# Two attention outputs behind one another on TensorE, and q's factor in its cast

## The chip, the cores and the metric

The kernel runs on one core of one Trainium2 chip. The metric is the device time of one execution in microseconds, the median of several runs. Everything that the profile shows comes from one profiled execution of the same program. PE is TensorE (PEld its weight loads), DVE is VectorE, ACT is ScalarE, POOL is GpSimd, SP is SyncE, which here only issues DMAs.

## The reference, cut to what matters

Attention with one added to the softmax denominator, then a feed-forward layer with the Mish-like gate. 8 batches, 12 heads, 448 positions, head width 64; the layer sees 3584 tokens of width 768, and its inner width is 2048.

```python
scores = scale * np.matmul(q, k.transpose(0, 1, 3, 2))          # scale = 1/8
m = np.max(scores, axis=-1, keepdims=True)
e = np.exp(scores - m)
attn = e / (np.sum(e, axis=-1, keepdims=True) + np.exp(-m) + 1e-09)
attn_out = np.matmul(attn, v)
x = attn_out.transpose(0, 2, 1, 3).reshape(3584, 768)
h = x @ w_in
g = h * np.tanh(np.log1p(np.exp(h)))                             # softplus inside
out = g @ w_out
```

## The kernel before, in words

**Pairs and units.** The 96 heads are taken two at a time: 48 pairs, six to a batch. Three pairs make a unit (`UNIT_PAIRS`), two units a batch; unit u has pairs 3u to 3u + 2, and `p0` is the first of them. Every instruction stands in the order in which the Python code writes it (the schedule is manual), so each engine runs its own instructions strictly in that order, and waits are put in by the framework from the data that instructions share.

**One pair** takes four steps. A step s computes scores of up to two blocks of 128 rows into the two banks of one of three PSUM tiles `sc` (PE, L327), takes the rows' maxima of both (DVE, L348), and exponentiates them into `en` (ACT, L361, with the sums collected at its side). The last step (s = 3) has one block only, so the second bank of its tile is free. `scores_ahead` keeps up to three steps of scores issued ahead of the exponentials; the scores of step n + 3 are therefore written right behind the exponentials of step n, into the tile that these set free. From pair 12 on the left operand is a block-diagonal copy of q, `qd` (`q_diag`, four buffers).

**The pair's output** (`av_pair`, L478) comes a unit later. It multiplies v by the transposed exponentials `eT`: eight matmuls, for two heads in two column halves of the array, into one PSUM bank, which VectorE copies to `xT` (L491). In the main units this output is written in front of the last score matmul of the pair three further on, in the free bank of the same `sc` tile (`av_with`, `bank=sc[:, 1, :]`): unit u computes the outputs of pairs p0 - 3, p0 - 2 and p0 - 1 at the last steps of its pairs p0, p0 + 1 and p0 + 2. `late` holds copies that are still to be written; `flush_late` writes them at the next chance, often the next step's start or the next part of the filler.

**The filler.** Between the steps PE works on the second matrix product of earlier batches (`mm2_part`, L567), in parts of sixteen matmuls of 384 or 192 columns. A part holds one of two PSUM tiles `mo` until VectorE has copied it to `o_sb` (L550). A list of weights, one for each of the unit's twelve steps, says which share of the unit's filler stands behind which step. After the twelve steps a unit has its share of the first matrix product (`mm1_mish`, L514 and L520), during which VectorE divides the exponentials by the denominators (`normalise`, L430), SP transposes them by DMA (L438, en to eT) and the next unit's first scores are issued.

**Loading.** SP issues the loads of q, k and v in float32 (L135), three buffers each. POOL casts them to bfloat16 (L186, `cast`). Up to pair 17 PE transposes q and k; from pair 18 (`BY_DMA_FROM`) two DMAs transpose three pairs at once (`turn_by_dma`, L197: k_cast to kT_all, q_cast to qT_all), and POOL writes both halves of each `qd` from qT_all, multiplying by 1/8 (L268). At a unit's first step POOL runs, in this order: a tiny copy that waits for the end of the previous normalisation (L714), the casts of v for pairs p0 - 2, p0 - 1 and p0, then k and q of the next unit's three pairs. The outputs of pairs p0 - 2 and p0 - 1 read v casts of this very list.

Of the kernel before, what the change touches and what calls it, by code (L numbers as in the profile page):

```python
# [12 lines left out]
ALU = mybir.AluOpType  # L13
AX = mybir.AxisListType

UNIT_PAIRS = 3
# [3 lines left out]
def kernel(  # L20
# [28 lines left out]
    STEPS = 4  # L49
# [65 lines left out]
    def flush_late():  # L115
        while late:
            late.popleft()()
# [10 lines left out]
    def load_pair(p, names="qkv"):  # L128
        if p >= N_PAIRS:
            return  # L130
        b, h0 = p // HP, (p % HP) * 2
        for nm in names:
            src = dict(q=q, k=k, v=v)[nm]
            t = ld_pool.tile([SP_, 2, NT * D], FP32, tag=f"{nm}_f", name=f"{nm}_f")
            nc.sync.dma_start(  # L135
                out=t, in_=src[b, h0 : h0 + 2].rearrange("h (p t) d -> p h (t d)", t=NT)
            )
            loaded.setdefault(p, {})[nm] = t
# [33 lines left out]
    def cast(p, names):  # L172
        if p >= N_PAIRS:
            return
        by_t = "p h (t d) -> p t h d"
        to = casted.setdefault(p, {})
        for nm in names:
            src = loaded[p].pop(nm)
            if nm != "v":
                to[nm] = (q_cast if nm == "q" else k_cast)[:, p % UNIT_PAIRS]  # L180
            else:
                to[nm] = bf_pool.tile([SP_, 2, NT * D], BF16, tag="v_bf", name="v_bf", bufs=7)
            if nm != "v":
                src = src.rearrange(by_t, t=NT)
            if p > 0 or nm == "v":
                nc.gpsimd.tensor_copy(out=to[nm], in_=src)  # L186
                continue
            cuts = (0, NT) if nm == "k" else (0, NT // 2, NT)
            for lo, hi in zip(cuts, cuts[1:]):
                nc.vector.tensor_copy(out=to[nm][:, lo:hi], in_=src[:, lo:hi])  # L190
# [42 lines left out]
    def evac_qk(p, act=False):  # L233
        if p >= N_PAIRS:
            return
        by_dma = p >= BY_DMA_FROM
        by = nc.gpsimd if by_dma else nc.vector
        kT = kT_all[:, p % (2 * UNIT_PAIRS)]
        (q_ps, k_ps), own = ((qT_all[:, p % UNIT_PAIRS], kT), []) if by_dma else qkT[p]
        mo_free.extend(own)  # L240
        q_reads = []
        qd = q_diag[p % len(q_diag)]
        if p < DIAG_FROM:
            qT = qd.rearrange("d i h r -> d (i h r)")[:, 0:S]
            qkT[p] = (qT, kT)
            if p == 0:
                nc.scalar.copy(kT, k_ps[:, 0:S])
                by_2 = sc_tiles[2][:, 0, :].bitcast(BF16)
                for ps, half in (q_ps, slice(0, S // 2)), (by_2, slice(S // 2, S)):
                    nc.vector.tensor_scalar(  # L250
                        out=qT[:, half], in0=ps[:, half], scalar1=SCALE, scalar2=None,
                        op0=ALU.mult,
                    )
                return
            if act:
                nc.scalar.mul(qT, q_ps[:, 0:S], SCALE)
            else:
                q_reads.append(nc.vector.tensor_scalar(
                    out=qT, in0=q_ps[:, 0:S], scalar1=SCALE, scalar2=None, op0=ALU.mult
                ))  # L260
        else:
            qkT[p] = (qd, kT)
            if p < DIAG_FROM + len(q_diag):
                nc.vector.memset(qd[0:64, :, 1, :], 0.0)
                nc.vector.memset(qd[64:128, :, 0, :], 0.0)
            for h in range(2):
                rows = slice(64 * h, 64 * h + 64)
                q_reads.append(by.tensor_scalar(  # L268
                    out=qd[rows, :, h, :],
                    in0=q_ps[rows, 0:S].rearrange("d (i r) -> d i r", i=QB),  # L270
                    scalar1=SCALE, scalar2=None, op0=ALU.mult,
                ))
        if by_dma:
            return
        if own and not act:
            nc.vector.tensor_copy(out=kT, in_=k_ps[:, 0:S])
        else:
            k_read = nc.scalar.copy(kT, k_ps[:, 0:S])
            if not own:
                apart(k_read, *q_reads)  # L280
# [26 lines left out]
    def scores(idx):  # L307

        p, s = divmod(idx, STEPS)
        if s == 0:  # L310
            if p < HP or p % UNIT_PAIRS == 0:
                for nm in ("negm", "sums", "expm", "den", "rden"):
                    stats[nm] = st_pool.tile([128, UNIT_PAIRS, NTILE], FP32, tag=nm, name=nm)
            at = 0 if p < HP else p % UNIT_PAIRS
            att[p] = {nm: t[:, at, :] for nm, t in stats.items()}
            att[p].update(en=en_bufs[p % N_EN], whole=dict(stats))
        st = att[p]
        qT, kT = qkT[p]
        kA, kB = kT[0:64, :], kT[64:128, :]
        sc = sc_tiles[idx % len(sc_tiles)]  # L320
        if s == STEPS - 1 and p in av_with:
            av_pair(av_with.pop(p), bank=sc[:, 1, :], beside=idx)
        if p >= DIAG_FROM:
            cols = tuple(range(2 * s, min(2 * s + 2, NTILE)))
            negm = st["negm"][:, cols[0] : cols[-1] + 1]
            for bk, i in enumerate(cols):
                nc.tensor.matmul(  # L327
                    sc[:, bk, 0:S], lhsT=qT[:, i].rearrange("d h r -> d (h r)"), rhs=kT,
                    start=True, stop=True,
                )  # L330
        elif s < 3:
            qa, qb = 128 * s, 64 + 128 * s
            nc.tensor.matmul(
                sc[:, 0, 0:S], lhsT=qT[0:64, qa : qa + 128], rhs=kA, start=True, stop=True
            )
            nc.tensor.matmul(
                sc[:, 1, 0:S], lhsT=qT[64:128, qb : qb + 128], rhs=kB, start=True, stop=True
            )
            cols, negm = (s, 4 + s), st["negm"][:, s : s + 5 : 4]
        else:  # L340
            nc.tensor.matmul(
                sc[0:64, 0, 0:S], lhsT=qT[0:64, 384:S], rhs=kA, start=True, stop=True
            )
            nc.tensor.matmul(
                sc[64:128, 0, 0:S], lhsT=qT[64:128, 0:64], rhs=kB, start=True, stop=True
            )
            cols, negm = (3,), st["negm"][:, 3:4]
        half_max[p] = nc.vector.tensor_reduce(  # L348
            out=negm, in_=sc[:, 0 : len(cols), 0:S], axis=AX.X, op=ALU.max, negate=True
        )  # L350
        st["sc", s] = (sc, cols)
# [250 lines left out]
            plan[u0 + 3] += [(g, 6, 2, 2)]  # L602


    weight = [5.2] + [1.0] * (steps - STEPS) + [0.4] * (STEPS - 1)

    LEAD = UNIT_PAIRS + 1
    LOAD_AT = (0, 3, 6)
# [61 lines left out]
    for u in range(UNITS_PER_B, N_UNITS + 2 * UNITS_PER_B):  # L670
        attn = u < N_UNITS
        filler = deque()
        for part in plan.get(u, []):
            filler.extend(mm2_part(*part))
        total, done, acc = sum(w for _, w in filler), 0, 0.0
        p0 = u * UNIT_PAIRS
        if attn and u >= first_mm2:
            av_with.update({p0 + i: p0 + i - UNIT_PAIRS for i in range(UNIT_PAIRS)})
        nxt = p0 + UNIT_PAIRS
        end = min(nxt, N_PAIRS) * STEPS  # L680

        for n in range(steps):
# [24 lines left out]
            if n in LOAD_AT and u <= first_mm2:  # L707
                at = p0 + LOAD_AT.index(n)
                load_pair(at + LEAD, "qk")
                load_pair(at + 1, "v")  # L710
                cast(at + LEAD - 1, "qk")
                cast(at, "v")
            elif n == 0 and u <= N_UNITS:
                nc.gpsimd.tensor_copy(  # L714
                    out=marks[0:1, 3, 0:2], in_=att[p0 - 1]["en"][0:1, NT - 1, NTILE - 1, 0:2]
                )
                for p_ in range(p0 - UNIT_PAIRS + 1, p0 + 1):
                    if "v" in loaded.get(p_, ()):
                        cast(p_, "v")
                for i in range(UNIT_PAIRS):  # L720
                    cast(nxt + i, "kq")
                turn_by_dma(nxt)
                load_pair(nxt + UNIT_PAIRS, "kq")
                for i in range(UNIT_PAIRS):
                    load_pair(p0 + 1 + i, "v")
            if s == 0 and u > first_mm2:
                evac_qk(nxt + pi)
            if n == steps - 1 and u >= first_mm2:
                for i in range(1, UNIT_PAIRS):
                    load_pair(nxt + UNIT_PAIRS + i, "kq")  # L730
            for pe, n0 in BY_PE.items():
# [27 lines left out]
        for f in range(FF_U):  # L759
# [6 lines left out]
            if f == 0:  # L766
                denominators(p0, UNIT_PAIRS)
                for p in todo if p0 < LATE_DIV else todo[:1]:
                    normalise(p, dma=p not in BY_PE)
            if f == 5 and u == UNITS_PER_B + 1:  # L770
                spread_rden(p0, copy=nc.scalar.copy)
            if f == 4:
# [42 lines left out]
```

## Time and profile before

| | |
|---|---|
| median of 3 runs | 471.48 us (470.95 to 472.93) |
| the profiled execution, whole | 475.91 us |
| its span, first to last instruction | 474.1 us |
| mean granted TensorE clock in it | 0.993 |
| busy: PE, DVE, ACT, POOL | 449.2, 347.5, 331.6, 180.8 us |
| DMA | 97.94 MB, mean 207 GB/s |
| one load of q, k or v | 224 KB, landing after 4.8 to 5.1 us (median) |

How to read it. A profile row such as "210.54 0.95 PE L478 MATMUL sc<-eT,v_bf 112*64 112x448 bf16 x8" is: start in us, time from the first start to the last end, engine, line, operation, output and inputs, shape, and how many instructions were merged. Matmuls overlap in the pipeline, so the distance from one row's start to the next is their cost on PE, not the second number. A bracket at a row's end tells how long the engine stood idle before it and whose end released it. In group rows the numbers behind the bar are total busy time and the mean of one in ns, then the idle time before them.

### The profile page before, as it was taken

The numbers are of one execution on the slowest core, as the hardware profiler recorded it, in microseconds if no ns is written. First come the engines' busy times: TensorE is split into PE (matmuls) and PEld (weight loads), VectorE is DVE, ScalarE is ACT, GpSimd is POOL, SyncE is SP. The second block draws the span as 40 slices with busy tenths as digits, with TensorE's granted clock in tenths as the row PEclk, the third lists the DMA queues.
The fourth block names the chain that finished last, engine by engine and source line by source line (L and its number), as shares of the span: only waits on it lengthen the run. The fifth ranks groups of instructions, "written<-read, shape, count | busy, mean of one in ns | idle before, by whom it ended". The sixth has DMA issues, their size and how long they took to land.

```text
span 474.1 us, 8841 instructions
## 1 busy us (share of the span) xinstructions
PE 449.2 (95%) x3051; PEld 245.8 (52%) x3051; DVE 347.5 (73%) x657; ACT 331.6 (70%) x877; POOL 180.8 (38%) x258
## 2 busy tenths in 40 slices
PE   7778888999889999999999999999999999999996
PEld 3344445555535555555555555555555555556563
DVE  5999738759859798989898888989798979421021
ACT  5998848879747887978686869687887869211300
POOL 4613609105126455455463644646464620100000
PEclk9999999999989999999999999999999999999999
DMA  8999999999999999999999999999999594921122
GB/s 253 228 115 244 220 216 209 174 214 252 185 239 280 222 273 231 261 250 230 259 233 287 212 224 242 282 233 268 217 273 235 155 213 128 225 76 33 35 57 77
DMA packets 232493, 97.94 MB, mean 207 GB/s; under 512 B 189312, under 2 KB 228992, under 8 KB 232448
## 3 DMA queue, kind: packets, MB, share of 16 engines
q1 hardware_dynamic: 224928, 91.06, 84.9%
q0 software_dynamic: 7488, 6.29, 9.2%
q8 instruction: 24, 0.39, 0.4%
q14 instruction: 21, 0.17, 0.1%
q10 hardware_dynamic: 32, 0.02, 0.0%
HBM read 45.61 MB, written 11.01 MB: 119 GB/s over the span
## 4 chain that ended last, share of the span: by engine, by line
PE 68%; ACT 6%; DVE 5%; DMA 3%; issue 1%; SPq 0%; DVEq 0%; ACTq 0%
PE mo L514 24%; PE mo L567 24%; PE sc L327 8%; PE sc L478 6%; ACT en L361 6%; DVE negm L348 4%; PE sc L514 4%; DMA eT<-en 3%; PE mo L478 1%; DVE xT L491 1%; PE mo L288 0%; DMA out_dram<-o_sb 0%; DVE o_sb L550 0%; PE sc L220 0%; DVE eT L453 0%
## 5 line engine op out<-in xcount | busy, mean ns | idle before, releaser
L361 ACT ACTIVATE en<-sc,negm 128x448 bf16<-128x448 f32 x336 | 208.8, 643 | 27.3 <-DVE negm L348 25.5
L348 DVE TENSOR_REDUCE negm<-sc 128x2 f32<-128x896 f32 x192 | 182.6, 970 | 50.2 <-PE sc L327 39.6
L567 PE MATMUL mo<-w_out_sb,gT 128*128 128x384 bf16 (+1 forms) x1024 | 167.4, 307 | 0.4 <-DVE rb L418 0.4
L514 PE MATMUL mo<-xT,w_in_sb 128*128 128x448 bf16 x672 | 139.0, 352 | 2.8 <-DMA w_in_sb<-in_moe_w_in_dram 2.6
L567 PEld LDWEIGHTS <-gT 128*128 128x128 bf16 x1024 | 96.6, 98 | 56.6 <-issue 2.9
L520 ACT ACTIVATE gT<-mo 128x448 bf16<-128x448 f32 x112 | 59.4, 543 | 82.2 <-PE mo L514 81.8
L514 PEld LDWEIGHTS <-w_in_sb 128*128 128x128 bf16 x768 | 74.0, 98 | 72.0 <-DMA w_in_sb<-in_moe_w_in_dram 3.8
L268 POOL TENSOR_SCALAR qd<-qT_all 64x448 bf16<-64x448 bf16 x60 | 80.1, 1335 | 61.7 <-DMA qT_all<-q_cast 32.6
L430 DVE TENSOR_SCALAR en<-en,rden 128x448 bf16<-128x448 bf16 x252 | 85.5, 413 | 0.5
L361 ACT ACTIVATION_READ_ACCUMULATOR en<-sc,negm 128x1 f32 x336 | 72.2, 215 | 0.0
L327 PE MATMUL sc<-kT_all,qd 128*128 128x448 bf16 x252 | 72.2, 356 | 0.0
L550 DVE COPY o_sb<-mo 128x384 f32<-128x384 f32 (+1 forms) x64 | 31.9, 498 | 48.3 <-PE mo L567 48.1
L478 PE MATMUL sc<-eT,v_bf 112*64 112x448 bf16 x336 | 40.2, 360 | 5.4 <-DMA eT<-en 3.6
L186 POOL CAST q_cast<-q_f 112x512 bf16<-112x512 f32 x47 | 28.6, 608 | 32.6 <-PE mo L409 18.6
L327 PEld LDWEIGHTS <-qd 128*128 128x128 bf16 x252 | 24.7, 98 | 29.2 <-issue 13.4
L714 POOL COPY marks<-en 1x2 bf16<-1x2 bf16 x12 | 2.1, 175 | 96.3 <-DVE en L430 96.3
L478 PEld LDWEIGHTS <-v_bf 112*64 112x64 bf16 x384 | 20.0, 109 | 24.1 <-issue 7.4
L186 POOL CAST k_cast<-k_f 112x512 bf16<-112x512 f32 x47 | 28.5, 607 | 0.6 <-DMA k_f<-in_k_dram 0.3
L186 POOL CAST v_bf<-v_f 112x512 bf16<-112x512 f32 x48 | 28.1, 605 | 1.5 <-DMA v_f<-in_v_dram 1.1
L514 PE MATMUL sc<-xT,w_in_sb 128*128 128x448 bf16 x96 | 20.8, 352 | 0.0
L491 DVE CAST xT<-sc 128x448 bf16<-128x448 f32 x33 | 20.3, 615 | 0.0
L520 ACT ACT_TABLE_LOAD x14 | 18.0, 1283 | 0.8 <-PE mo L514 0.3
(63 smaller groups left out, 245.2 us busy)
## 6 DMA issues: line engine op xcount, KB each, us to landing
k_f<-in_k_dram SPq DMA_DIRECT2D x48, 224.0 KB, 5.0
q_f<-in_q_dram SPq DMA_DIRECT2D x48, 224.0 KB, 4.8
v_f<-in_v_dram SPq DMA_DIRECT2D x48, 224.0 KB, 5.1
w_in_sb<-in_moe_w_in_dram POOLq DMA_DIRECT2D x12, 256.0 KB, 10.7
w_out_sb<-in_moe_w_out_dram POOLq DMA_DIRECT2D x8, 384.0 KB, 13.3
out_dram<-o_sb SPq DMA_DIRECT2D x7, 336.0 KB, 4.1
out_dram<-o_sb SPq DMA_DIRECT2D x8, 288.0 KB, 5.1
out_dram<-o_sb SPq DMA_DIRECT2D x8, 240.0 KB, 3.7
```

The costliest lines, as they stand in the source:

```text
L186: nc.gpsimd.tensor_copy(out=to[nm], in_=src)
L268: q_reads.append(by.tensor_scalar(out=qd[rows, :, h, :], in0=q_ps[rows, 0:S].rearrange("d (i r) -> d i r", i=QB), scalar1=SCALE, scalar2=N ...
L327: nc.tensor.matmul(sc[:, bk, 0:S], lhsT=qT[:, i].rearrange("d h r -> d (h r)"), rhs=kT, start=True, stop=True,)
L348: half_max[p] = nc.vector.tensor_reduce(out=negm, in_=sc[:, 0 : len(cols), 0:S], axis=AX.X, op=ALU.max, negate=True)
L361: e = nc.scalar.activation(out=st["en"][:, :, c, 0:SP_], in_=sc[:, bk, 0:S].rearrange("q (j c) -> q j c", j=NT), func=AF.Exp, bias=st["neg ...
L430: nc.vector.tensor_scalar(out=en[:, :, i, 0:SP_], in0=en[:, :, i, 0:SP_], scalar1=st["rden"][:, i : i + 1], scalar2=None, op0=ALU.mult,)
L478: mm = nc.tensor.matmul(av[h * 64 : (h + 1) * 64, 0:S], lhsT=v_bf[:, h, j * D : (j + 1) * D], rhs=e_h, start=(j == 0), stop=(j == NT - 1),)
L491: read = nc.vector.tensor_copy(out=to, in_=av[:, 0:S])
L514: nc.tensor.matmul(h_ps[:, 0:S], lhsT=w_in_sb[:, dm, ff * 128 : (ff + 1) * 128], rhs=xT[b][:, dm, :], start=(dm == 0), stop=(dm == DM_T - 1),)
L520: nc.scalar.activation(out=gT[:, ff, b % 2 * S : b % 2 * S + S], in_=h_ps[:, 0:S], func=AF.Mish)
L550: nc.vector.tensor_copy(out=o_sb[:, cols.start : cols.start + n_dve], in_=st["o"][:, 0:n_dve])
L567: nc.tensor.matmul(st["o"][:, 0:n_cols], lhsT=gT[:, ff, i * 128 : (i + 1) * 128], rhs=w_out_sb[:, ff, cols], start=(ff == 0), stop=(ff == ...
```

## The change

From unit 5 to unit 15 (pairs 15 to 47) the first of a unit's three outputs no longer stands at the first pair's last step. It stands at the second pair's last step, directly in front of the second output, in a `mo` tile of its own, and its copy is written at once. The third output stays at the third pair's last step. In these units the filler's weights are changed.

From pair 18 on the factor 1/8 moves from POOL's writes of `qd`, which become plain copies, into POOL's cast of q, which becomes a `tensor_scalar`. At a unit's first step POOL casts k and q of the next unit first, and then v.

In unit 4 the loads of q and k for pairs 19 and 20 are issued behind the first normalisation and its transpose instead of ahead of them, at the last step.

```diff
@@ cast
+            if nm == "q" and p >= BY_DMA_FROM:
+                nc.gpsimd.tensor_scalar(
+                    out=to[nm], in0=src, scalar1=SCALE, scalar2=None, op0=ALU.mult
+                )
+                continue
             if p > 0 or nm == "v":
                 nc.gpsimd.tensor_copy(out=to[nm], in_=src)
                 continue
@@ evac_qk
-                q_reads.append(by.tensor_scalar(
-                    out=qd[rows, :, h, :],
-                    in0=q_ps[rows, 0:S].rearrange("d (i r) -> d i r", i=QB),
-                    scalar1=SCALE, scalar2=None, op0=ALU.mult,
+                q_h = q_ps[rows, 0:S].rearrange("d (i r) -> d i r", i=QB)
+                if by_dma:
+                    nc.gpsimd.tensor_copy(out=qd[rows, :, h, :], in_=q_h)
+                    continue
+                q_reads.append(nc.vector.tensor_scalar(
+                    out=qd[rows, :, h, :], in0=q_h, scalar1=SCALE, scalar2=None, op0=ALU.mult,
                 ))
@@ scores
         if s == STEPS - 1 and p in av_with:
-            av_pair(av_with.pop(p), bank=sc[:, 1, :], beside=idx)
+            *in_mo, in_sc = av_with.pop(p)
+            for other in in_mo:
+                av_pair(other)
+                flush_late()
+            av_pair(in_sc, bank=sc[:, 1, :], beside=idx)
@@ the weights
-    weight = [5.2] + [1.0] * (steps - STEPS) + [0.4] * (STEPS - 1)
+    weight_first = [5.2] + [1.0] * (steps - STEPS) + [0.4] * (STEPS - 1)
+    weight_joint = [5.2] + [1.4] * 3 + [1.0] * 4 + [0.6] + [0.4] * 3
@@ the units' loop
+        weight = weight_joint if first_mm2 < u < N_UNITS else weight_first
         p0 = u * UNIT_PAIRS
         if attn and u >= first_mm2:
-            av_with.update({p0 + i: p0 + i - UNIT_PAIRS for i in range(UNIT_PAIRS)})
+            done_at = (0, 1, 2) if u == first_mm2 else (1, 1, 2)
+            for i, at in enumerate(done_at):
+                av_with.setdefault(p0 + at, []).append(p0 + i - UNIT_PAIRS)
...
+                for i in range(UNIT_PAIRS):
+                    cast(nxt + i, "kq")
                 for p_ in range(p0 - UNIT_PAIRS + 1, p0 + 1):
                     if "v" in loaded.get(p_, ()):
                         cast(p_, "v")
-                for i in range(UNIT_PAIRS):
-                    cast(nxt + i, "kq")
                 turn_by_dma(nxt)
...
-            if n == steps - 1 and u >= first_mm2:
+            if n == steps - 1 and u > first_mm2:
                 for i in range(1, UNIT_PAIRS):
                     load_pair(nxt + UNIT_PAIRS + i, "kq")
...
                 for p in todo if p0 < LATE_DIV else todo[:1]:
                     normalise(p, dma=p not in BY_PE)
+                if u == first_mm2:
+                    for i in range(1, UNIT_PAIRS):
+                        load_pair(nxt + UNIT_PAIRS + i, "kq")
```

More of the change, by code (lines that the diff above doesn't have):

```diff
@@ L236, in evac_qk @@
         by_dma = p >= BY_DMA_FROM
-        by = nc.gpsimd if by_dma else nc.vector
         kT = kT_all[:, p % (2 * UNIT_PAIRS)]
```

## The prediction

> **What bounds the kernel now.** I read the page first, then the stretches, then the order of time on each engine.
>
> ```profile
> span 474.1 us, 8841 instructions
> PE 449.2 (95%) x3051; PEld 245.8 (52%) x3051; DVE 347.5 (73%) x657; ACT 331.6 (70%) x877; POOL 180.8 (38%) x258
> ...
> 120.00:146.00 26.00, 22.42 (x141) 12.04 (x140) 18.15 (x35) 16.41 (x45) 6.38 (x10) 0.93 1.20 214
> ...
> 197.00:222.40 25.40, 25.30 (x158) 13.87 (x157) 22.85 (x44) 20.39 (x56) 13.67 (x18) 1.00 1.04 259
> ```
>
> The columns of a stretch are its length, busy PE, PEld, DVE, ACT and POOL, then granted clock, DMA share, GB/s. A unit (three pairs; unit 8 here) takes 25.4 us and PE is busy in 25.3 of it: PE bounds, and every wait put into PE's stream is lost for good. VectorE, at 22.85 us, is close behind. Only unit 5 (120 to 146 us) has a hole.
>
> PE in unit 8 (pairs 24 to 26), with the steps that the change moves; L478 is an attention output, L327 scores, L567 the filler:
>
> ```profile
> 207.19 3.41 PE L567 MATMUL mo<-w_out_sb,gT 128*128 128x384 bf16 x20
> 210.54 0.95 PE L478 MATMUL sc<-eT,v_bf 112*64 112x448 bf16 x8
> 211.42 0.36 PE L327 MATMUL sc<-kT_all,qd 128*128 128x448 bf16 x1
> ...
> 214.70 0.81 PE L567 MATMUL mo<-w_out_sb,gT 128*128 128x384 bf16 x4
> 215.47 0.95 PE L478 MATMUL sc<-eT,v_bf 112*64 112x448 bf16 x8
> 216.35 0.36 PE L327 MATMUL sc<-kT_all,qd 128*128 128x448 bf16 x1
> 216.55 0.81 PE L567 MATMUL mo<-w_out_sb,gT 128*128 128x384 bf16 x4
> 217.20 0.54 PE L327 MATMUL sc<-kT_all,qd 128*128 128x448 bf16 x2
> 217.57 0.81 PE L567 MATMUL mo<-w_out_sb,gT 128*128 128x384 bf16 x4
> ...
> 220.39 0.95 PE L478 MATMUL sc<-eT,v_bf 112*64 112x448 bf16 x8
> ```
>
> Starts to starts: four filler matmuls take 0.65 us, two scores 0.38, one 0.19, an attention output 0.88. Going into an output costs more: 214.70 + 0.65 is 215.35, and it starts at 215.47, 0.12 late; and its 0.88 is 0.13 above four pairs of 448 columns at 0.19 each (two matmuls run side by side). So a separate output costs some 0.24 us of changing over.
>
> The third output starts where a chain ends, not where PE is ready:
>
> ```profile
> 216.81 0.62 DVE L348 TENSOR_REDUCE negm<-sc 128x1 f32<-128x448 f32 x1 [0.29 <-PE sc L327]
> 217.35 0.62 DVE L491 CAST xT<-sc 128x448 bf16<-128x448 f32 x1
> 217.89 3.10 DVE L348 TENSOR_REDUCE negm<-sc 128x2 f32<-128x896 f32 x3
> ...
> 219.00 0.63 ACT L361 ACTIVATE en<-sc,negm 128x448 bf16<-128x448 f32 x1 [0.51 <-DVE negm L348]
> ...
> 220.14 0.20 ACT L361 ACTIVATION_READ_ACCUMULATOR en<-sc,negm 128x1 f32 x1
> ```
>
> Last score of the second pair (216.35), its maximum (216.81), the output's copy (217.35), the third pair's first maximum (217.89), its two exponentials (219.00 to 220.34), then the third output in the bank they free (220.39): 4.04 us. PE's own work there is about 3.87, so 0.17 is already waited. PE and this chain are level.
>
> **Joining the outputs.** In units 5 to 15 the first output leaves the front of the first pair's last score and stands directly before the second. One change-over goes: 11 x 0.24 = 2.6 us. No matmul is added. What follows, in unit 8, from the score that now comes first (210.44, the 20 fillers at 0.1625 from 207.19):
>
> The filler weights put two more filler matmuls (0.33 us) between the first and the second pair's last score, and two fewer behind. PE asks for the second pair's first scores at 211.3 but their tile is free only when the first pair's second step is exponentiated:
>
> ```profile
> 211.29 0.21 ACT L361 ACTIVATION_READ_ACCUMULATOR en<-sc,negm 128x1 f32 x1
> ```
>
> It ends at 211.50, PE goes on at 211.55: 0.26 us waited, which the output hid before. The first output now needs a mo bank. In even units the filler part that held it has just ended, the copy out of it stands behind a maximum on VectorE, and by the same latencies PE waits another 0.13. So the second pair's last score starts at 216.35 - 0.24 + 0.26 + 0.13 + 0.33 = 216.83. From there PE has 3.54 us of work to the third output (a score 0.19, ten fillers 1.63, six half-wide ones 0.49, three times two scores 1.14, changing over 0.09); the chain still takes 4.04. The third output starts at 220.87 instead of 220.39, with the same work done: **+0.48 us in an even unit**, although the gap went.
>
> An odd unit:
>
> ```profile
> 235.88 0.95 PE L478 MATMUL sc<-eT,v_bf 112*64 112x448 bf16 x8
> ...
> 241.69 0.36 PE L327 MATMUL sc<-kT_all,qd 128*128 128x448 bf16 x1
> ...
> 245.74 0.95 PE L478 MATMUL sc<-eT,v_bf 112*64 112x448 bf16 x8
> ...
> 243.23 1.08 DVE L348 TENSOR_REDUCE negm<-sc 128x2 f32<-128x896 f32 x1
> 244.23 0.55 DVE L550 COPY o_sb<-mo 128x384 f32<-128x384 f32 x1
> 244.69 2.08 DVE L348 TENSOR_REDUCE negm<-sc 128x2 f32<-128x896 f32 x2
> ```
>
> Without the output in front, its first pair's last score starts at 235.71. The same steps (-0.24, 0.24 waited, 0.33 of filler) bring the second pair's last score to 242.02. But the filler part now ends two matmuls behind it, so that in VectorE's order the copy to o_sb (0.46, 244.23 to 244.69) comes ahead of the third pair's first maximum instead of behind it: the chain, 4.05 now, becomes 4.51, against 3.70 of work on PE (fourteen fillers). Third output at 246.53 instead of 245.74: **+0.79**. The first output's own copy has slack.
>
> **q's factor in its cast, and v's casts behind k's and q's.** This sits on POOL:
>
> ```profile
> L268 POOL TENSOR_SCALAR qd<-qT_all 64x448 bf16<-64x448 bf16 x60 | 80.1, 1335 | 61.7 <-DMA qT_all<-q_cast 32.6 <-PE sc L327 13.5 <-PE sc L478 12.0
> L186 POOL CAST q_cast<-q_f 112x512 bf16<-112x512 f32 x47 | 28.6, 608 | 32.6 <-PE mo L409 18.6 <-DMA q_f<-in_q_dram 13.9
> ...
> L389 POOL CAST hl<-rden 128x7 bf16<-128x7 f32 x6 | 1.1, 191 | 12.7 <-DVE rden L385 12.2 <-PE mo L409 0.5
> ...
> 210.27 0.17 POOL L714 COPY marks<-en 1x2 bf16<-1x2 bf16 x1 [5.76 <-DVE en L430]
> 210.40 1.70 POOL L186 CAST v_bf<-v_f 112x512 bf16<-112x512 f32 x3
> 212.05 0.60 POOL L186 CAST k_cast<-k_f 112x512 bf16<-112x512 f32 x1
> 212.60 0.60 POOL L186 CAST q_cast<-q_f 112x512 bf16<-112x512 f32 x1
> ...
> 235.71 1.70 POOL L186 CAST v_bf<-v_f 112x512 bf16<-112x512 f32 x3
> ```
>
> Sixty multiplies become copies and thirty casts become multiplies of 112x512. No row shows that one. Bounds: 0.608 us, the plain cast of the same data, and the multiply at L268's rate: 0.18 us fixed (7 columns take 0.191), (1.335 - 0.18) / 448 = 2.58 ns a column, so 1.50 us for 512. I take 1.50, as the same operation; casts follow each other 0.05 closer than they last.
>
> What waits: the second output reads the v cast first among this unit's three. It is done at 211.0 now and used at 215.47. Afterwards, from 210.40: three k casts at 0.55, three q at 1.45, then v in 0.60: 217.0. PE is there at 216.0. The output starts at 217.07, the score behind it at 217.95, the third output 4.04 later at 221.99: **+1.60 in an even unit**, the 0.48 included. Odd, with the casts from 235.71: the second output at 242.38, the score at 243.26, plus 4.51 is 247.77: **+2.03**. Up to a multiply of about 1.1 us nothing is added to 0.48 and 0.79. Units 6 to 14 cast both; unit 15 has no k and q left, unit 5's second output uses an older v.
>
> [...]
>
> The copies into qd, between 0.53 (the cast's rate) and 1.33 us, are covered either way: at 1.33 they are ready in time now. With POOL shorter there, VectorE's normalisation is less disturbed; PE waits for no eT in steady units, so I price this at nothing.
>
> ```profile
> 215.00 1.92 SPq L197 DMA_TRANSPOSE kT_all<-k_cast  x1
> 217.03 1.55 SPq L197 DMA_TRANSPOSE qT_all<-q_cast  x1
> ```
>
> SP's transposes of k and q are issued at these times now, behind the unit's eT. Their third casts would be done at 215.0 (k) and 216.4 (q): no shift.
>
> **The loads of pairs 19 and 20.** Unit 5:
>
> ```profile
> 132.66 1.38 PE L478 MATMUL sc<-eT,v_bf 112*64 112x448 bf16 x8 [3.58 <-DMA eT<-en]
> ...
> 144.12 0.95 PE L478 MATMUL sc<-eT,v_bf 112*64 112x448 bf16 x8
> ...
> L438 SPq DMA_TRANSPOSE eT<-en x3: 3738/3873/12086, 118.3 to 134.4; - x3
> ...
> DMA to landing us min/median/max: 6.4/6.8/14.3
> ```
>
> The first of the three takes 12.1 us to issue and lands at 132.6, 14.3 after 118.3; PE waits 3.58 us for it. Four loads now go behind this transpose instead of ahead, so it lands sooner, by an estimated 2 to 3 us. The second stays behind all of the same transfers: issued at 130.4 and landed 6.4 later, at 136.8; afterwards 137 to 139, because the queue runs empty for an estimated 1 to 2 us before 118.3. With the join the second output follows the first at once. PE gets there at 132.66 - 3.58 + 4.3 (fillers and scores) + 0.9 (first output) = 134.3 and waits for the second eT instead. At 138, the third output comes at 138 + 0.88 + 4.51 = 143.4 instead of 144.12: **-0.7**, between -2.7 (136) and +0.8 (139.5). The 3.58 us hole is moved rather than closed.
>
> **Sum.** 5 x 1.60 + 4 x 2.03 + 0.79 (unit 15) - 0.7 = +16.2 us. The profiled execution took 475.91 (its span and 1.8 around it): 492.1. The runs' median is 4.4 lower, in the whole run: 471.48 + 16.2 = **487.7 us**.
>
> **Rivals.** *The multiply is quick*, at most 1.1 us: no v wait, only the chain is left, 5 x 0.48 + 5 x 0.79 - 0.7 = +5.7, 477.2 us. For it: plain casts run at 0.608. Against: L268. Between 1.1 and 1.45 us lie 478 to 487. [...]
> *Faster: the change-over decides.* The multiply is quick and the third output finds its bank free, because VectorE, relieved of POOL or in another order, gets through the chain in under 3.5 us: -2.6, and -0.7 to -2.7 in unit 5: 466.2 to 468.2. Against it stands 4.04 us in rows that the change doesn't touch; it decides only where at least 0.5 us of that goes.
> *The parts cancel*: chain +0.3 a unit, unit 5 at its best: within 2.4 us of 471.5.
>
> **How the numbers follow.** The multiply near 1.5: 0.50; in between: 0.10; quick with the chain: 0.18; cancelling: 0.06; faster: 0.16. A measurement tells about 0.5% (2.4 us) from no change. Slower 0.78, same 0.06, faster 0.16. Likeliest case alone: 483 to 492 (multiply 1.4 to 1.6, unit 5's bounds). Leaving out the faster case and a tail: 471 to 491.5.
>
> **What would show it.** POOL's q multiply by its mean; PE waiting for POOL's v cast before the second output, 9 times about 1 us; the third output waiting for ACT 0.4 to 0.8 us in every unit from 6; units of 26.9 (even) and 27.3 us (odd) instead of 25.3; unit 5's wait at its second output, for eT. A multiply under 1.1 us, or third outputs without a wait, would make the forecast wrong.

## The result and the profile after

| | before | after |
|---|---|---|
| median | 471.22 us (469.15 to 472.93) | 487.44 us (486.12 to 491.94) |
| the profiled execution, whole | 475.91 us | 491.72 us |
| ratio of the times, 95% interval | | 1.0375 (1.0317 to 1.0433) |

The change makes the kernel slower by 3.75%, 16.2 us between the medians; 487.7 us was forecast. Some executions of a kernel take over 1.5% longer than its fastest: the medians here and below count them, the ratios leave them out. The page after:

```profile
span 489.6 us, 8838 instructions
...
PE 452.6 (92%) x3051; PEld 248.4 (51%) x3051; DVE 329.6 (67%) x657; ACT 334.3 (68%) x877; POOL 161.4 (33%) x258
```

VectorE and GpSimd are *less* busy (347.5 and 180.8 us before). TensorE has the same 3051 matmuls, 3.4 us more busy time, and its share falls from 95 to 92%. So most of the time was not added as work; it went into waits. The place is read from stretches cut from third output to third output, units 8 and 9, first of the kernel before and then of the one after (length, PE, PEld, DVE, ACT, POOL):

```profile
sum 50.65, PE 50.55 PEld 27.63 DVE 44.88 ACT 40.43 POOL 26.76; mean PE 25.27 PEld 13.81 DVE 22.44 ACT 20.22 POOL 13.38
```

```profile
197.25:224.16 26.91, 25.36 (x151) 13.59 (x151) 20.13 (x43) 20.46 (x54) 10.90 (x16) 1.00 0.91 228
224.16:251.55 27.39, 25.49 (x163) 14.28 (x163) 20.56 (x44) 20.36 (x54) 12.57 (x20) 1.00 0.92 230
sum 54.30, PE 50.86 PEld 27.88 DVE 40.70 ACT 40.82 POOL 23.47; mean PE 25.43 PEld 13.94 DVE 20.35 ACT 20.41 POOL 11.73
```

The lengths are those forecast, 26.9 us for an even and 27.3 for an odd unit (before 25.30 and 25.35); two units take 3.65 us more, at a granted clock of 1.00 in both kernels. In unit 8 TensorE's order of time has two holes that were not there (first the two joint outputs, then the score, then the third output), and GpSimd's shows why the first is there:

```profile
217.32 0.95 PE L488 MATMUL mo<-eT,v_bf 112*64 112x448 bf16 x8
219.23 0.95 PE L488 MATMUL sc<-eT,v_bf 112*64 112x448 bf16 x8 [0.97 <-POOL v_bf L191]
220.11 0.36 PE L337 MATMUL sc<-kT_all,qd 128*128 128x448 bf16 x1
...
224.16 0.95 PE L488 MATMUL sc<-eT,v_bf 112*64 112x448 bf16 x8 [0.43 <-ACT en L371]
```

```profile
212.43 0.17 POOL L728 COPY marks<-en 1x2 bf16<-1x2 bf16 x1 [13.02 <-DVE en L440]
212.55 0.60 POOL L191 CAST k_cast<-k_f 112x512 bf16<-112x512 f32 x1
213.12 1.48 POOL L186 TENSOR_SCALAR q_cast<-q_f 112x512 bf16<-112x512 f32 x1
...
218.58 1.71 POOL L191 CAST v_bf<-v_f 112x512 bf16<-112x512 f32 x3
```

The first of the three v casts ends at about 219.18; without a wait the second output starts 0.76 us after the first (experiment 1), which is 218.1 here. Over the whole run, in the view of waits (us in all, times, longest):

```profile
PE sc L488 <- POOL v_bf L191: 9.2, 9, 1.1
PE sc L488 <- ACT en L371: 7.0, 13, 0.7
PE sc L488 <- DMA eT<-en: 1.9, 1, 1.9
```

Nine waits for v, as many as there are units 6 to 14. The multiply and its neighbours among the groups of instructions:

```profile
L440 DVE TENSOR_SCALAR en<-en,rden 128x448 bf16<-128x448 bf16 x252 | 64.1, 332 | 0.5
...
L186 POOL TENSOR_SCALAR q_cast<-q_f 112x512 bf16<-112x512 f32 x30 | 44.4, 1478 | 0.0
L274 POOL COPY qd<-qT_all 64x448 bf16<-64x448 bf16 x60 | 33.3, 556 | 29.6 <-DMA qT_all<-q_cast 24.7
```

### The profile page after: what moved, and what is told of

It is laid out like the page before. It is cut to its first block, busy times and chain, and to the rows that moved or that the text cites. A ratio compares the mean times of both kernels' runs of the same rounds, so it can differ in the third digit from the quotient of the medians.

```text
span 489.6 us, 8838 instructions
## 1 busy us (share of the span) xinstructions
PE 452.6 (92%) x3051; PEld 248.4 (51%) x3051; DVE 329.6 (67%) x657; ACT 334.3 (68%) x877; POOL 161.4 (33%) x258
## 4 chain that ended last, share of the span: by engine, by line
issue 28%; PE 25%; POOL 18%; DMA 5%; DVE 4%; ACT 2%; SPq 1%; POOLq 0%; DVEq 0%
PE mo L577 10%; PE mo L524 8%; POOL q_cast L186 8%; POOL qd L274 6%; DMA qT_all<-q_cast 5%; POOL k_cast L191 3%; DVE negm L358 2%; PE sc L488 2%; ACT en L371 2%; PE sc L337 2%; PE sc L524 1%; PE mo L488 1%; POOL v_bf L191 1%; DVE o_sb L560 1%; SPq L448 1%
## 5 line engine op out<-in xcount | busy, mean ns | idle before, releaser
L371 ACT ACTIVATION_READ_ACCUMULATOR en<-sc,negm 128x1 f32 x336 | 70.2, 209 | 0.0
L440 DVE TENSOR_SCALAR en<-en,rden 128x448 bf16<-128x448 bf16 x252 | 64.1, 332 | 0.5
L488 PE MATMUL sc<-eT,v_bf 112*64 112x448 bf16 x248 | 30.0, 363 | 18.2 <-POOL v_bf L191 9.2
L186 POOL TENSOR_SCALAR q_cast<-q_f 112x512 bf16<-112x512 f32 x30 | 44.4, 1478 | 0.0
L274 POOL COPY qd<-qT_all 64x448 bf16<-64x448 bf16 x60 | 33.3, 556 | 29.6 <-DMA qT_all<-q_cast 24.7
L337 PEld LDWEIGHTS <-qd 128*128 128x128 bf16 x252 | 24.6, 98 | 28.0 <-issue 13.0
L191 POOL CAST q_cast<-q_f 112x512 bf16<-112x512 f32 x17 | 10.5, 616 | 25.6 <-PE sc L337 17.2
```

Of the source, the lines that this page charges most:

```text
L186: nc.gpsimd.tensor_scalar(out=to[nm], in0=src, scalar1=SCALE, scalar2=None, op0=ALU.mult)
L274: nc.gpsimd.tensor_copy(out=qd[rows, :, h, :], in_=q_h)
L337: nc.tensor.matmul(sc[:, bk, 0:S], lhsT=qT[:, i].rearrange("d h r -> d (h r)"), rhs=kT, start=True, stop=True,)
L371: e = nc.scalar.activation(out=st["en"][:, :, c, 0:SP_], in_=sc[:, bk, 0:S].rearrange("q (j c) -> q j c", j=NT), func=AF.Exp, bias=st["neg ...
L440: nc.vector.tensor_scalar(out=en[:, :, i, 0:SP_], in0=en[:, :, i, 0:SP_], scalar1=st["rden"][:, i : i + 1], scalar2=None, op0=ALU.mult,)
L488: mm = nc.tensor.matmul(av[h * 64 : (h + 1) * 64, 0:S], lhsT=v_bf[:, h, j * D : (j + 1) * D], rhs=e_h, start=(j == 0), stop=(j == NT - 1),)
```

## The experiments

All kernels in one table. "Two units" is the distance between the third outputs of units 7 and 9 in the profiled execution, repeated within 0.1 us by each later two units up to unit 15 (in the kernel after and in 3 up to unit 13: unit 15 casts no k and q, and units 14 and 15 together take 53.04 and 52.25 us there). It tells more than the medians, since the executions of one kernel scatter by one or two per cent here (what is known of that is said at the fifth experiment).

| kernel | ratio to before (95%) | two units, us |
|---|---|---|
| before | 1 | 50.65 |
| after | 1.0375 (1.0317 to 1.0433) | 54.30 |
| 1 after, v cast first | 1.0123 (1.0031 to 1.0216) | 51.88 |
| 2 after, q's cast plain | 1.0168 (1.0031 to 1.0305) | 51.88 |
| 3 before + factor in q's cast, v last | 1.0325 (1.0247 to 1.0403) | 53.83 |
| 4 before + joint outputs | 1.0182 (1.0083 to 1.0281) | 51.90 |
| 5 before + later loads | 0.9996 (0.9942 to 1.0051) | 50.64 |
| 6 joint outputs, old weights | 1.0158 (1.0071 to 1.0245) | 52.21 |
| 7 as 6, copy later | 1.0178 (1.0116 to 1.0241) | 52.80 |
| 8 before + copy later | 1.0050 (1.0005 to 1.0095) | 51.23 |
| 9 as 4, copy later | 1.0109 (1.0051 to 1.0166) | 51.65 |
| 10 filler moved, copy later | 1.0028 (0.9971 to 1.0085) | 50.99 |
| 11 filler moved | 1.0107 (1.0033 to 1.0181) | 51.51 |
| 12 filler moved less, copy later | 0.9989 (0.9952 to 1.0027) | 50.93 |

**1. The changed kernel with v's casts first.**

```diff
-                for i in range(UNIT_PAIRS):
-                    cast(nxt + i, "kq")
                 for p_ in range(p0 - UNIT_PAIRS + 1, p0 + 1):
                     if "v" in loaded.get(p_, ()):
                         cast(p_, "v")
+                for i in range(UNIT_PAIRS):
+                    cast(nxt + i, "kq")
```

> The changed kernel with one order changed: on GpSimd the three casts of v stand ahead of the casts of k and q again, the multiply still in q's cast. My theory (the multiplies make v's casts late, and the second attention output stands waiting for them): v is cast about 4 us earlier than the second output is due, the wait of about 1.1 to 1.4 us between the first and the second output goes in the nine units that have it, and the time falls by 9 x 1.2 = about 10.6 us to 476 to 478 us; the shorter steps from the third output remain (about +0.5 and +0.8 us a unit). [...] Rival B (k's and q's turning on the DMA queue, now later, is what the next unit then waits for): 480 or more, with a new wait for qT or kT.

Measured: 478.81 us median, a little above the band I gave; two units 51.88. GpSimd does the same multiplies (1.478 us each), and v is ready long before the outputs of unit 8:

```profile
211.59 1.70 POOL L191 CAST v_bf<-v_f 112x512 bf16<-112x512 f32 x3
...
216.35 0.95 PE L488 MATMUL mo<-eT,v_bf 112*64 112x448 bf16 x8
217.11 0.95 PE L488 MATMUL sc<-eT,v_bf 112*64 112x448 bf16 x8
...
222.04 0.95 PE L488 MATMUL sc<-eT,v_bf 112*64 112x448 bf16 x8 [0.43 <-ACT en L371]
```

The second output follows the first at once; the third still waits. 2.42 us of the 3.65 for two units have gone. That the multiply itself or the load on GpSimd is the cost falls with this (the multiplies are all still there, while the ratio goes from 1.0375 to 1.0123), and so does rival B: no wait for qT or kT appears on TensorE.

**2. The changed kernel with q's factor back in the writes of `qd`**, the order of the casts kept.

```diff
-            if nm == "q" and p >= BY_DMA_FROM:
-                nc.gpsimd.tensor_scalar(out=to[nm], in0=src, scalar1=SCALE, ...)
-                continue
...
-                    nc.gpsimd.tensor_copy(out=qd[rows, :, h, :], in_=q_h)
+                    nc.gpsimd.tensor_scalar(out=qd[rows, :, h, :], in0=q_h, scalar1=SCALE, ...)
```

> The changed kernel with q's factor back in the two writes of q's operand, so that q's cast is a plain copy again; the new order of the casts (k and q ahead of v) is kept. My theory: v's casts end about 0.9 us x 3 earlier, before the second output is due, so the wait goes: 476 to 478 us. Rival A (the order of the casts alone makes v late): stays at 485 to 488. Rival C (taking the factor out of the operand writes is a gain that this undoes): between, 479 to 482.

Measured: 481.25 us median with a wide interval, the profiled execution 480.24; two units 51.88, as in 1. With six plain casts ahead of it v still comes in time (casts from 212.78, the second output of unit 8 at 214.99 without a wait):

```profile
212.78 1.74 POOL L186 CAST v_bf<-v_f 112x512 bf16<-112x512 f32 x3
```

So neither the order alone nor the multiply alone makes the wait: it takes both. Undoing either is worth the same 2.42 us for two units. The median lies above the band I gave and within rival C's. The steady units decide between the two: with the factor back in the writes of `qd` (here) or in the cast (1) they take the same 51.88 us, so C falls, and what is long in the profiled execution is unit 5 (25.9 us, below).

**3. The multiply and the order alone**, the outputs where they were before (the diffs of `cast`, `evac_qk` and the casts' order from the change, nothing else).

> The kernel before, with only the factor in q's cast and the casts of k and q ahead of v's; the three outputs stand where they stood. My theory: the second output stands behind the score after the unit's first pair in step, so the wait for v comes at another place, but v's last casts are as late: about 1.2 to 1.6 us in nine units, 482 to 486 us. If the wait needs the joint outputs too, 471 to 474.

Measured: 485.51 us; two units 53.83. The wait stands at the second output's old place, now 1.6 us long:

```profile
212.75 0.95 PE L484 MATMUL sc<-eT,v_bf 112*64 112x448 bf16 x8 [1.56 <-POOL v_bf L191]
```

The joint outputs are not needed for it. They even shorten it, since they bring TensorE to the second output later: 3.18 us (this) and 1.25 us (the next) make 4.43 for two units, and together they cost 3.65.

**4. The joint outputs and their weights alone.**

```diff
+            *in_mo, in_sc = av_with.pop(p)
+            for other in in_mo:
+                av_pair(other)
+                flush_late()
+            av_pair(in_sc, bank=sc[:, 1, :], beside=idx)
...
+    weight_joint = [5.2] + [1.4] * 3 + [1.0] * 4 + [0.6] + [0.4] * 3
...
+            done_at = (0, 1, 2) if u == first_mm2 else (1, 1, 2)
```

> The kernel before, with only the joint outputs and their weights. My theory: no wait for v; the chain from the score through the two copies to the third output is longer than the work beside it by 0.5 us in even and 0.8 us in odd units from the sixth, less 1.9 us in the fifth: 5 x 0.5 + 6 x 0.8 - 1.9, about +5 us, 475 to 477 us. Rival D (a change-over saved, 0.24 us a unit, decides, and the chain has cover): 468 to 469. Rival E (the joint outputs cost as much as the whole change): 484 or more.

Measured: 477.81 us; two units 51.90, +0.46 in unit 8 and +0.79 in unit 9. The chain of unit 8 in this kernel's order of time: the second pair's last score; its maximum, the copy of the second output and the third pair's maxima; the third pair's first exponential; the third output.

```profile
214.65 0.36 PE L331 MATMUL sc<-kT_all,qd 128*128 128x448 bf16 x1
...
215.12 0.62 DVE L352 TENSOR_REDUCE negm<-sc 128x1 f32<-128x448 f32 x1 [0.50 <-PE sc L331]
215.66 0.61 DVE L495 CAST xT<-sc 128x448 bf16<-128x448 f32 x1
216.19 2.08 DVE L352 TENSOR_REDUCE negm<-sc 128x2 f32<-128x896 f32 x2
...
217.31 0.63 ACT L365 ACTIVATE en<-sc,negm 128x448 bf16<-128x448 f32 x1 [0.74 <-DVE negm L352]
...
218.70 0.95 PE L482 MATMUL sc<-eT,v_bf 112*64 112x448 bf16 x8 [0.43 <-ACT en L365]
```

From 214.65 to 218.70 are 4.05 us. Is the change-over saved at all? Take each matmul's start less the one before it, and count what it is above the step that the same two kinds have undisturbed (0.19 between scores, 0.16 in the filler, 0.26 from filler to output). These waits add up to 0.25 us for the two units before, to 2.03 here. TensorE's own work is then 50.65 - 0.25 = 50.40 before and 51.90 - 2.03 = 49.87 here: 0.53 us less, two change-overs at the 0.24 I had. The saving is real, and 1.78 us of new waits spend it.

**5. The later loads of pairs 19 and 20 alone.**

```diff
-            if n == steps - 1 and u >= first_mm2:
+            if n == steps - 1 and u > first_mm2:
...
+                if u == first_mm2:
+                    for i in range(1, UNIT_PAIRS):
+                        load_pair(nxt + UNIT_PAIRS + i, "kq")
```

> The kernel before, with only the later loads of q and k for pairs 19 and 20. Theory of the prediction: the transposed weights of pair 13 land earlier in unit 5, where TensorE waited 3.6 us for them, and nothing else moves: 468 to 470 us, with unit 5 (from its start to the third output) 2 to 3.6 us shorter and every later unit at 50.65 us for two. Rival F (the runs so far: with late loads that wait was 3.8 and 4.0 us, and 0.8 us in a run without them): the later loads meet the weights of the second stage at the queue and the wait does not get shorter: 471 to 474. Rival G: that wait differs from one execution to the next whatever the loads are.

Measured: 473.95 us, ratio 0.9996: no difference, where 468 to 470 us was expected. The order of time on SP's queue around unit 5, of this kernel and then of the third one, which loads early:

```profile
115.75 9.81 SPq L438 DMA_TRANSPOSE eT<-en  x1
125.66 0.53 SPq L135 DMA_DIRECT2D k_f<-in_k_dram  x1
...
127.79 9.57 SPq L438 DMA_TRANSPOSE eT<-en  x2
```

```profile
116.05 16.95 SPq L444 DMA_TRANSPOSE eT<-en  x3
```

The four loads now stand between the first transpose and the second. The first lands 11.9 us after it was issued instead of 14.3, but the first output still waits 1.59 us for it, and the second output pays:

```profile
136.42 1.71 PE L478 MATMUL sc<-eT,v_bf 112*64 112x448 bf16 x8 [3.75 <-DMA eT<-en]
```

From the 900th matmul (at the end of unit 4) to unit 5's third output the four profiled executions with later loads take 23.3, 25.9, 26.2 and 26.3 us; the ten without take 19.3 to 25.1, before itself 24.6. Three of the four are longer than all ten, so this stage speaks for a loss rather than a gain, though the times of the 5th kernel show neither. What sets the length within 19 to 26 us isn't settled: with one profiled execution of each kernel, the placing of the loads and the state of the DMA queues can't be told apart. It is the only stage, beside the start (the 900th matmul comes between 116.4 and 120.1 us), that differs by microseconds between kernels that hardly differ there; whether it also makes the executions of one kernel differ, no trace shows. From unit 5's third output to the last matmul the first, second and fourth kernels take 331.04, 331.05 and 331.14 us, before 325.24.

**6. Joint outputs with the old weights** (the diff of 4 without `weight_joint`).

> The kernel before, with the joint outputs but the old weights of the filler. My theory (the chain from the second pair's last score to the third output sets the time, and the new weights moved that score later): the joint outputs with the new weights cost 1.2 us for two units; with the old ones the score comes about 0.33 us earlier, so two units take 50.65 + 0.5 = about 51.2 us instead of 51.9: 472 to 475 us. Rival H (weights change nothing): 51.9 us for two units, 476 to 478. Rival D (with the old weights the change-over saved shows): 50.2 us, 468 to 469.

Measured: 479.84 us; two units 52.21. All three theories missed. With the old weights the filler has just begun a new part when the first output asks for a `mo` bank, so in even units the output waits for the copy of the part before:

```profile
214.74 0.95 PE L482 MATMUL mo<-eT,v_bf 112*64 112x448 bf16 x8 [1.06 <-DVE o_sb L554]
```

This is what the new weights are good for: with them the part is one step further on, and that wait is 0.1 us.

**7, 8 and 9. The second output's copy behind the next maximum**, to take it out of the chain: with the joint outputs and old weights (7), in the kernel before alone (8), with the joint outputs and new weights (9).

```diff
+            if p % UNIT_PAIRS == 1 and p > 15:
+                after_max.append(late.pop())
...
+            behind_max = list(after_max)
+            after_max.clear()
             scores_ahead(end)
+            for copy_out in behind_max:
+                copy_out()
```

> The joint outputs with the old weights, and the copy of the second output put behind the next maximum on VectorE instead of ahead of it. If that copy (0.62 us, of which 0.54 in the chain) is the link that makes the chain longer than TensorE's work, the third output is reached earlier and the change-over saved shows: two units in 50.2 to 50.5 us, 467 to 470 us. If the chain is bound by ScalarE's exponentials instead, the copy's place changes nothing and the time is that of the joint outputs with old weights: 51.1 us for two units, 472 to 475.

> The kernel before, with only the copy of the second output put behind the next maximum. The chain there is 4.04 us against 3.87 us of TensorE's own work, so at most 0.17 us a unit is to be had: two units in 50.3 to 50.65 us, 468 to 471.5 us. If the copy's later place delays something behind it (the o_sb copy or a maximum), two units take more than 50.65.

> Joint outputs with the new weights, and the copy of the second output put behind the next maximum on VectorE. My theory of the joint outputs' 1.2 us for two units: 0.4 and 0.8 us are the chain into the third output (gaps of 0.68 and 1.07 us instead of 0.26), 0.26 a unit is a wait of a score for its tile, and 0.48 is gained by the change-overs. Without the copy in the chain the two gaps go, the 0.26 stay: two units in 50.6 to 50.8 us, 470 to 474 us. If the chain is not the cause, 51.9 us for two units.

Measured: 52.80, 51.23 and 51.65 us for two units; 50.2 to 50.5, 50.3 to 50.65 and 50.6 to 50.8 were expected if the copy's place helps, so in none did it help as hoped. The 7th has the 6th's wait for `mo`, and more behind it. In the 9th the third output no longer waits (it starts 0.20 and 0.28 us after the filler, against 0.68 and 1.07 in the 4th), and nearly nothing is gained: the copy now releases its `sc` bank late, and the third pair's third scores wait for that bank. In the waits of units 8 to 14 of the 9th:

```profile
PE sc L334 <- DVE xT L498: 1.1, 4, 0.3
```

The 8th, without joint outputs, loses 0.58 us for two units in this way. So neither place tried for the copy on VectorE is free: ahead of the maximum it delays the third output, behind it the third scores.

**10, 11 and 12. The filler moved to where the first output was**, so that TensorE does not run ahead there. With the late copy and 2.0 of weight moved (10), with the copy where it was (11), with the late copy and 1.0 moved (12).

```diff
+    weight_joint = [7.2] + [1.0] * 3 + [0.0] * 2 + [1.0] * 3 + [0.4] * 3   # 10 and 11
+    weight_joint = [6.2] + [1.0] * 4 + [0.0] + [1.0] * 3 + [0.4] * 3       # 12
```

> Joint outputs, the late copy of the second output, and weights that put 2.0 more at the unit's first step (about the time of the output that left it) and take it from the two steps at the joint outputs, so that the scores are asked for when they were before. If the wait for the tile (0.26 us a unit) comes from the output that left the first step, it goes, and the change-over saved is left: two units in 50.0 to 50.3 us, 467 to 470 us. If not, as with the new weights: 50.6 or more.

> The same weights (2.0 more at the first step, none at the joint outputs), the copy of the second output where it was, ahead of the next maximum. The chain from the second pair's last score to the third output is then 4.04 us in even units against about 3.87 us of TensorE's work, as before the change: two units in 50.2 to 50.7 us, 468 to 471.5 us. If the weights do not matter, 51.9 us.

> The late copy with weights between: 1.0 more at the first step, none at the step behind the joint outputs. The wait of the scores for their tiles is halved at best: two units in 50.2 to 50.6 us, 468 to 471 us.

Measured: 50.99, 51.51 and 50.93 us for two units, all above the bands hoped for (50.0 to 50.3, 50.2 to 50.7 and 50.2 to 50.6); the ratios of the 10th and 12th can't be told from 1. Most of the joint outputs' cost can be won back by placing, but no version is faster than before. Waits by starts in two units: about 1.4, 1.9 and 1.1 us. In the 11th the third output waits for the exponentials again. In the 12th, the best, the joint outputs start within 0.1 us of their time, and what is left is the copy's wait, the third pair's third scores in unit 8 behind the copy at 217.89:

```profile
217.89 0.62 DVE L498 CAST xT<-sc 128x448 bf16<-128x448 f32 x1
...
218.57 0.55 PE L334 MATMUL sc<-kT_all,qd 128*128 128x448 bf16 x2 [0.26 <-DVE xT L498]
```

## Why the prediction was right, step by step

**The multiply: right.** Taken at 1.50 us between 0.61 and 1.50, measured 1.478. From the list's first cast to the end of the first v cast I had 6.6 us; after, it is 212.55 to 219.18, 6.63. With it falls the rival of a quick multiply, at most 1.1 us. The 1.50 carries L268's rate over from a bfloat16 input of 64x448 to a float32 input of 112x512; no row of the kernel before shows that step, and it was the author's estimate. Measured, the two agree within 2%.

**The wait for v: right, in both its size and its conditions.** Forecast 1.07 (even) and 1.24 us (odd) in units 6 to 14; between the starts of the two joint outputs there are 1.15 and 1.23 us more than in a unit without the wait. That it needs the multiply *and* the order, and no join, is shown by experiments 1 to 3.

**The chain and the third output: right.** Forecast +0.48 and +0.79 us; the joint outputs alone give +0.46 and +0.79. With the wait for v, +1.60 and +2.03 were forecast; the third outputs move by +1.61 in even units, +2.04 to +2.15 in odd ones, and +0.78 in unit 15 (+0.79). In odd units the reason is the forecast one too: in unit 9 of the fourth kernel the copy to `o_sb` stands ahead of the third pair's maxima, where before it stood behind the first of them.

```profile
241.33 0.61 DVE L495 CAST xT<-sc 128x448 bf16<-128x448 f32 x1
241.86 0.55 DVE L554 COPY o_sb<-mo 128x384 f32<-128x384 f32 x1
242.33 3.08 DVE L352 TENSOR_REDUCE negm<-sc 128x2 f32<-128x896 f32 x3
```

The rival "the chain alone is left" (+5.7 us: +6.35 from unit 6 on, -0.7 in unit 5) is what the first, second and fourth experiments ran: from unit 5's third output on they take 5.8 to 5.9 us more than before. Nearly all that is short of 6.35 is unit 6, which takes 0.06 or 0.07 us more in them instead of 0.48.

**Unit 6: the term was mis-sized.** I gave it unit 8's +1.60, and it took +1.28. Unit 6 was 25.63 us long before, 0.33 more than unit 8; the forecast did not take it by itself. In it the third output already began 0.68 us after the filler's last start, 0.42 more than undisturbed.

**Unit 5: the sign is luck, and two terms were mis-sized.** Forecast -0.7 (between -2.7 and +0.8), measured -1.27 in the one profiled execution. The wait moves to the second output, as foreseen, but it is 1.94 us and not the 3.7 of the forecast: that eT is there at 136.3 instead of 138. Against this, the way from the second output to the third took 6.53 us instead of 0.88 + 4.51 = 5.39:

```profile
136.32 1.56 PE L488 MATMUL sc<-eT,v_bf 112*64 112x448 bf16 x8 [1.94 <-DMA eT<-en]
137.82 0.56 PE L337 MATMUL sc<-kT_all,qd 128*128 128x448 bf16 x1
138.17 1.49 PE L577 MATMUL mo<-w_out_sb,gT 128*128 128x384 bf16 x4
...
142.85 0.95 PE L488 MATMUL sc<-eT,v_bf 112*64 112x448 bf16 x8 [0.24 <-ACT en L371]
```

```profile
132.00:134.00 2.00, 2.00 (x15) 1.04 (x15) 2.00 (x3) 1.88 (x7) 2.00 (x3) 1.00 1.27 290
137.50:138.50 1.00, 1.00 (x7) 0.29 (x4) 0.02 (x1) 0.00 (x0) 0.00 (x0) 0.50 1.27 290
138.50:139.50 1.00, 1.00 (x5) 0.49 (x4) 1.00 (x2) 0.36 (x1) 0.00 (x0) 0.50 1.24 280
```

Behind the wait the granted clock is 0.50, from 1.00 ahead of it, and four filler matmuls take 1.28 us from start to start instead of 0.65. The forecast priced that at nothing, though the kernel before has it too (0.50 from 134 to 136 us, behind its own wait of 3.58). That the later loads gain anything is not borne out: alone they gave no difference, and before's own unit 5 is the second longest of the ten that load early, so that one comparison with it says little on the sign.

**The change-over: right in size (0.24 forecast, 0.27 by the starts), and it decided nothing,** since the chain has no cover. The faster rival asked for a chain of under 3.5 us. Experiments 9, 10 and 12 took the third output's wait away and ended at 1.0109, 1.0028 and 0.9989: it would not have come true that way either.

**The sum.** Forecast +16.2; the last matmul starts 15.5 us later (484.89 against 469.37), and the medians are 16.2 apart. By unit: -1.27, +1.28, four times about +2.07, four times +1.61, +0.78: 15.5. The agreement of the medians to the decimal is luck: units 5 and 6 are off by -0.6 and -0.3 us, and the median of the kernel before moved between 471.2 and 472.3 us from one set of runs to the next.

## What to carry to other kernels

When an operation moves from behind a wait to ahead of a list on an engine that works through its list in order, as GpSimd does here (k, q and v one after another from 212.55 to 220.29 us of the kernel after), price the whole list up to the item that somebody needs next: three multiplies of 1.48 us a unit cost nothing on GpSimd, at a third of the span, and 11 us on TensorE, until v was cast first. Where PE's work and a chain through two other engines are level, taking PE work out of that stretch, or moving a copy within the chain, may only rename the wait, as in experiments 6 to 9; look at which bank the next user needs before counting a gain.

## What the runs showed of the hardware that had not been expected

VectorE's `normalise` (128x448, bfloat16) takes 413 ns on average where GpSimd multiplies into `qd` beside it and 332 ns in the changed kernel, and 333 in the third experiment; in the second, which has those multiplies back, it is 402. The copies into `qd` stand in the multiplies' place and take 0.556 us instead of 1.335.

```profile
L430 DVE TENSOR_SCALAR en<-en,rden 128x448 bf16<-128x448 bf16 x252 | 85.5, 413 | 0.5
```

The mean hides three groups. One by one in the trace of the kernel before, the 146 that no multiply overlaps take 317 to 339 ns. The 62 that lie across a multiply's start or end take 504 to 708. Of the 44 that begin and end while one multiply runs, 37 take 323 to 336, no more than alone (29 of 33 in the second experiment). In the changed kernel no multiply lies beside any, and all 252 take 326 to 338. So a multiply that runs beside it need not make `normalise` longer: the 37 took no longer inside a multiply of 1.34 us than without one. What delays the 62, and the other seven of the 44 (404 to 611), stays open, and the profile's times on GpSimd are rough.

VectorE's gain, some 18 us of busy time, moved no end: in experiments 1 and 2 it is busy for 41.38 and 45.62 us of two units, and both take 51.88. Not the sum of its list bounds these units, only the order of three of its instructions does.
